# The weight sums of the first pair on VectorE, moved behind the outputs of one product of the down projection and behind the activation sums

## Chip, cores, metric

One core of a Trainium2 chip runs the whole kernel. The metric is device time in microseconds for one execution, on that core. Times of one kernel are compared with runs of the kernel before made on the same chip in the same rounds. A profile is one execution of the same program.

## The reference, cut to what matters

```python
x = A_x                                    # 2048 rows of 1024, bfloat16
h = x + attention(layernorm(x)) @ wo       # sliding, dilated, 32 heads
n = layernorm(h)
h2 = h + ((n @ w_gate) * (n @ w_up)) @ w_down   # 1024 -> 3584 -> 1024
```

The second half is the part at issue. Rows are handled in chunks of 512. Chunk 0 is computed plainly. Chunk 1's down projection, and the gate, up and down projections of chunks 2 and 3 together, use a Strassen-like scheme: seven products of quarter blocks instead of eight, at the price of sums and differences of blocks on the other engines.

## The kernel before

The place where the change is made lies at two thirds of the span. Chunk 1's down projection ends there, and the pairs of gate and up products for chunks 2 and 3 begin. Products accumulate in tiles called ex and ey (two of each) in PSUM, the memory into which the matmuls write; `dprod` is a product, 14 matmuls for each tile:

```python
def result(c, rows, t, hf, ps, sc, other, lo=0, n=TC):
    cols = bass.ds(hf * 512 + lo, n)
    nc.vector.scalar_tensor_tensor(rows[:, cols], ps[:, bass.ds(lo, n)], sc,
                                   rows[:, cols] if other is None else other[:, bass.ds(lo, n)], ALU.mult, ALU.add)   # L792
    nc.sync.dma_start(outf[bass.ds(c * TC + t * 128, 128), cols], rows[:, cols])                                      # L794
```

For pair 0, the scaled weights are made by ScalarE and the four weight sums by VectorE (GpSimd makes those of all other pairs):

```python
def weight_sums(n, eng=nc.gpsimd):
    raw = pair["w", n]
    wt = wpool.tile([128, KO, 2, 256], F16, tag="w", name=f"ws_{n}")
    if n == 0:
        nc.scalar.activation(wt[:], raw[:], ACTF.Copy, scale=scale_gu.s)              # L654
    else:
        nc.vector.tensor_scalar(wt[:], raw[:], scale_gu.s, None, ALU.mult)            # L656
    sw = wpool.tile([128, 2, 4, 4, 128], F16, tag="w", name=f"sw_{n}")
    # ... a11, a21, a12, a22 are quarters of wt
        eng.tensor_tensor(sw[:, i, 0], a21, a22, ALU.add)                             # L661
        eng.tensor_tensor(sw[:, i, 1], sw[:, i, 0], a11, ALU.subtract)                # L662
        eng.tensor_tensor(sw[:, i, 2], a11, a21, ALU.subtract)                        # L663
        eng.tensor_tensor(sw[:, i, 3], a12, sw[:, i, 1], ALU.subtract)                # L664
```

The activation sums read the transposed, normalized rows of both chunks, l2 (chunk 2) and l3 (chunk 3), which the DMA queue transposes in eight transfers (in the profile of before they are issued one after the other, the last at 507.7 us, and that one lands 3.3 us later):

```python
def activation_sums(l2, l3, room):
    b11, b12, b21, b22 = l2[:, 0:4, :], l3[:, 0:4, :], l2[:, 4:8, :], l3[:, 4:8, :]
    # ... t1 to t4 are parts of room (the tile prodx)
    nc.vector.tensor_tensor(t1, b12, b11, ALU.subtract)                               # L672
    nc.vector.tensor_tensor(t2, b22, t1, ALU.subtract)                                # L673
    nc.vector.tensor_tensor(t3, b22, b12, ALU.subtract)                               # L674
    nc.vector.tensor_tensor(t4, b21, t2, ALU.subtract)                                # L675
```

And the order in which they are called, which is the order on each engine (the kernel schedules by hand):

```python
for t in range(4):
    ln_rows(3, t, l3)                      # ScalarE makes a row block, the DMA queue transposes it (L870)
sub([dn["kx"], dn["vx"]], dn["21"], dn["11"])
weight_sums(0, nc.vector)                  # <- the call that moves
retire(2)
et = att.tile([128, TC], F32, tag="t3", name="et")
for q in range(2):
    dprod(ex[q], q, EF["21"], fcells(dn["12"]), False)
    nc.vector.tensor_tensor(et[:], p5t[:, q, :], hs1[2 + q][:, 512:1024], ALU.add)    # L978
    result(1, hs1[2 + q], 2 + q, 1, ex[q], dn["inv"], et)
retire(1)
activation_sums(l2, l3, dn["px"])
for q in range(2):
    dprod(ey[q], q, EF["12"], fcells(dn["22"]), False)
    nc.vector.tensor_tensor(p5t[:, q, :], p5t[:, q, :], hs1[q][:, 512:1024], ALU.add) # L984
    result(1, hs1[q], q, 1, ey[q], dn["inv"], p5t[:, q, :])
for q in range(2):
    dprod(ex[q], q, EF["22"], fcells([dn["kx"], dn["vx"]]), False)                    # "second ex product"
    result(1, hs1[2 + q], 2 + q, 0, ex[q], dn["inv"], None)
# ... then pair_block(0): groups px, pv, py, pz of four matmuls each
```

The second ex product adds to the same PSUM tile that the first output reads, so it must wait for that output: 3.18 us in the profile of before. In `pair_block(0)` the first pv group takes a PSUM bank that the ey 0 output frees, and the second pv group one that the second output of ex 0 frees: in the profile after the change each of them starts about 0.05 us after that output ends (520.78 after 520.73, 522.89 after 522.83).

## Time and profile before

| | before |
|---|---|
| time, median of 3 runs | 783.46 us (782.1 to 784.1) |
| span of the profile | 779.9 us |
| TensorE busy | 766.8 us, 98% |
| longest wait of TensorE for another engine | 3.2 us, at the second ex product |
| longest wait of VectorE nearby | 4.44 us, for ScalarE's scaling |

In the timelines each row is start, duration, engine, line, operation, output, inputs, shape and count; a bracket at the end is idle time of the engine just before the row and what ended it. A matmul of 512 columns lasts 0.379 us but starts 0.216 us after the one before it, so rows of TensorE overlap and distances are best taken from start to start.

### The profile page before, as it was taken

How to read it: one execution, taken by the hardware profiler on the slowest of the kernel's cores; microseconds unless marked ns; L12 is line 12 of the kernel's file. 1: busy time of each engine (PE TensorE's matmuls, PEld its weight loads, DVE VectorE, ACT ScalarE, POOL GpSimd, SP SyncE). 2: the span in 40 equal slices, each digit the busy share in tenths (PEclk: the TensorE clock that was granted, in tenths of full speed). 3: DMA queues.
4: the chain of work that ended last, by engine and by line, in shares of the span. 5: the costliest groups of instructions: out<-in, count | busy, mean ns of one | idle time of the engine just before them, and what ended most of it. 6: DMA issues, size and time to landing. Idle time of an engine off the chain costs nothing.

```text
span 779.9 us, 10436 instructions
## 1 busy us (share of the span) xinstructions
PE 766.8 (98%) x3648; PEld 355.0 (46%) x3707; DVE 614.9 (79%) x805; ACT 473.5 (61%) x1028; POOL 142.4 (18%) x152
## 2 busy tenths in 40 slices
PE   8999999999999999999999999989999999999997
PEld 6544444444444444444444444434444444444444
DVE  6629999999899998999979989975553444579862
ACT  5627445313576652966769799836677677788240
POOL 0000000010000200002000001008778677600000
PEclk9999999999999999999999999999999999999999
DMA  8999693896955868858555492824332323730001
GB/s 272 260 236 209 169 274 90 262 274 173 341 174 186 297 215 234 270 189 270 195 163 195 133 313 75 183 74 110 106 99 64 108 67 97 255 123 28 1 27 55
DMA packets 181605, 133.86 MB, mean 172 GB/s; under 512 B 79024, under 2 KB 174384, under 8 KB 179504
## 3 DMA queue, kind: packets, MB, share of 16 engines
q1 hardware_dynamic: 177968, 111.17, 50.1%
q0 software_dynamic: 3584, 22.02, 8.1%
q8 instruction: 29, 0.48, 0.3%
q14 instruction: 24, 0.20, 0.1%
HBM read 104.86 MB, written 22.02 MB: 163 GB/s over the span
## 4 chain that ended last, share of the span: by engine, by line
PE 88%; DVE 9%; ACT 1%; issue 1%; DMA 1%; SPq 0%; DVEq 0%
PE ps L392 20%; PE pu L392 12%; PE pg L392 12%; PE dx L787 6%; PE pz L680 6%; PE acc L626 6%; PE py L680 6%; PE px L680 6%; PE wo L513 4%; PE pv L680 3%; PE dy L787 3%; DVE h L834 1%; PE ps L355 1%; PE ex L787 1%; DVE prodx L780 1%
## 5 line engine op out<-in xcount | busy, mean ns | idle before, releaser
L392 PE MATMUL ps<-lnT,w_qkv 128*128 128x512 bf16 x721 | 158.9, 379 | 0.8
L392 PEld LDWEIGHTS <-w_qkv 128*128 128x128 bf16 x736 | 71.9, 98 | 85.9
L392 PE MATMUL pu<-lnT,w_wu 128*128 128x512 bf16 x438 | 105.1, 379 | 0.6
L392 PE MATMUL pg<-lnT,w_wg 128*128 128x512 bf16 x440 | 105.1, 379 | 0.4
L306 ACT CAST sg<-ps 128x512 bf16<-128x512 f32 x96 | 54.8, 590 | 54.4 <-PE ps L392 51.1
L475 DVE TENSOR_TENSOR pv<-vD,at 128x4096 bf16<-128x4096 bf16 x32 | 72.5, 2287 | 0.3
L432 DVE TENSOR_TENSOR prod<-qD,kD 128x4096 bf16<-128x4096 bf16 x32 | 72.3, 2284 | 0.1
L680 PEld LDWEIGHTS <-sw 128*128 128x128 f16 x448 | 43.8, 98 | 53.2 <-issue 0.4
L392 PEld LDWEIGHTS <-w_wg 128*128 128x128 bf16 x448 | 43.8, 98 | 52.9
L392 PEld LDWEIGHTS <-w_wu 128*128 128x128 bf16 x448 | 43.8, 98 | 52.9
L596 ACT CAST us<-pu 128x512 bf16<-128x512 f32 x56 | 33.2, 593 | 41.1 <-PE pu L392 38.7
L680 PE MATMUL px<-lnT,ws 128*128 128x512 bf16 x212 | 53.1, 379 | 0.6
L680 PEld LDWEIGHTS <-ws 128*128 128x128 f16 x336 | 32.9, 98 | 39.6
L626 PE MATMUL acc<-w_wd,gs 128*128 128x512 bf16 x219 | 48.2, 379 | 0.3
L487 POOL DMA_DIRECT2D od<-oD x4 | 2.2, 544 | 252.3 <-DVE oD L485 162.5
L661 POOL TENSOR_TENSOR sw<-ws 128x512 f16<-128x512 f16 x26 | 30.0, 1154 | 87.6 <-PE py L680 80.4
L591 ACT CAST gs<-pg 128x512 bf16<-128x512 f32 x56 | 32.9, 587 | 11.4 <-PE pg L392 9.3
L185 ACT ACTIVATE rs<-mv,eps 128x1 f32<-128x1 f32 (+1 forms) x25 | 7.4, 297 | 50.3 <-DVE mv L182 47.1
L434 DVE TENSOR_TENSOR prod<-prod 128x4096 bf16<-128x4096 bf16 x16 | 36.6, 2288 | 0.3
L541 ACT ACTIVATE junkd<-w_wd 128x512 bf16<-128x512 bf16 x56 | 34.3, 613 | 0.0
L626 PEld LDWEIGHTS <-gs 128*128 128x128 bf16 x224 | 21.9, 98 | 26.4
L697 ACT COPY py<-px 128x512 f32<-128x512 f32 x28 | 16.0, 570 | 29.6 <-PE px L680 29.6
(304 smaller groups left out, 1398.0 us busy)
## 6 DMA issues: line engine op xcount, KB each, us to landing
w_wg<-in_B_w_gate_dram SPq DMA_DIRECT2D x14, 1024.0 KB, 6.6
w_wu<-in_B_w_up_dram SPq DMA_DIRECT2D x14, 1024.0 KB, 5.3
w_wd<-in_B_w_down_dram SPq DMA_DIRECT2D x8, 896.0 KB, 7.4
w_pair<-in_B_w_gate_dram SPq DMA_DIRECT2D x14, 512.0 KB, 4.0
w_pair<-in_B_w_up_dram SPq DMA_DIRECT2D x14, 512.0 KB, 5.2
w_wo<-in_A_wo_dram SPq DMA_DIRECT2D x6, 1024.0 KB, 8.4
w_qkv<-in_A_wqkv_dram SPq DMA_DIRECT2D x5, 1024.0 KB, 9.1
kd<-sg SPq DMA_DIRECT2D x32, 144.0 KB, 2.9
```

What stands on the lines that cost most here:

```text
L306: nc.scalar.copy(sg[:, HB:HB + TC], ps[:])
L392: nc.tensor.matmul(ps[:], lhsT=wt[:, ko, bass.ts(j, 128)], rhs=rhs[:, ko, :], start=(ko == 0), stop=(ko == KO - 1))
L432: nc.vector.tensor_tensor(prod[:, j], qD[:], kD[:, :, o:o + SUB], ALU.mult)
L434: nc.vector.tensor_tensor(prod[:, :, 0:16], prod[:, :, 0:16], prod[:, :, 16:32], ALU.add)
L475: nc.vector.tensor_tensor(pv[:, j], vD[:, :, o:o + SUB], at[:, w, None, :].to_broadcast((128, DH, SUB)), ALU.mult)
L513: nc.tensor.matmul(ps[:], lhsT=oTs[c][:, kk, t, :], rhs=wts["wo", c, hf][:, kk, :], start=(kk == 0), stop=(kk == KO - 1))
L541: nc.scalar.activation(junk, src, ACTF.Abs, accum_out=self.l1[:, k:k + 1])
L591: nc.scalar.copy(gs[:], pg[:])
L596: nc.scalar.copy(us[:], pu[:])
L626: nc.tensor.matmul(acc[t][:], lhsT=hT[f][:, bass.ts(t, 128)], rhs=wts["wd", c, hf, b][:, j, :], start=(f == 0), stop=(f == NF - 1))
L680: nc.tensor.matmul(ps[:], lhsT=lhs[:, ko, :], rhs=rhs[:, ko, :], start=(fresh and ko == 0), stop=(ko == 3), skip_group_check=not fresh)
L787: nc.tensor.matmul(ps[:, bass.ds(lo, n)], lhsT=lhs[k][:, bass.ts(q, 128)], rhs=rhs[k][:, bass.ds(lo, n)], start=(fresh and k == 0), stop=( ...
```

## The change

The intent is to let the outputs of the ex product, which need nothing from the weight scaling, go ahead of the weight sums, which do. The call moves behind the activation sums as well. No operation is added or removed.

```diff
     sub([dn["kx"], dn["vx"]], dn["21"], dn["11"])
-    weight_sums(0, nc.vector)
     retire(2)
     et = att.tile([128, TC], F32, tag="t3", name="et")
     for q in range(2):
@@
     retire(1)
     activation_sums(l2, l3, dn["px"])
+    weight_sums(0, nc.vector)
     for q in range(2):
         dprod(ey[q], q, EF["12"], fcells(dn["22"]), False)
```

## The prediction

> **What bounds the kernel now.** I read the page first, then the waits of TensorE over the whole span, then the chain of work that ended last, then the timelines of TensorE, VectorE, ScalarE and the DMA queue around the edited lines. From the page:
>
> ```profile
> span 779.9 us, 10436 instructions
> ...
> PE 766.8 (98%) x3648; PEld 355.0 (46%) x3707; DVE 614.9 (79%) x805; ACT 473.5 (61%) x1028; POOL 142.4 (18%) x152
> ...
> PEclk9999999999999999999999999999999999999999
> ```
>
> TensorE is busy 98% of the span at full clock, so only its 13 us of idle time can be won by a change that removes no matmul. The list of waits says where TensorE stands still for another engine (columns: us in total, times, longest):
>
> ```profile
> PE ex L787 <- DVE h L792: 3.2, 1, 3.2
> PE warm_ps L300 <- DVE warm L286: 1.2, 1, 1.2
> ...
> PE pv L680 <- DVE h L792: 0.2, 1, 0.2
> ```
>
> The longest wait of TensorE in the whole kernel is one of 3.2 us, for the output instruction at line 792; it is the one the change is about. The 0.2 us at the bottom is a few microseconds later in the same stage. TensorE's timeline there (start, duration, engine, line, what, and in brackets the idle time before):
>
> ```profile
> 509.70 1.67 PE L787 MATMUL ey<-lx,gs 128*128 128x512 f16 x7
> 514.56 1.67 PE L787 MATMUL ex<-kx,gs 128*128 128x512 f16 x7 [3.18 <-DVE h L792]
> ```
>
> and VectorE's:
>
> ```profile
> 503.96 2.02 DVE L780 TENSOR_TENSOR vx<-w_dn,w_dn 128x3584 f16<-128x3584 f16 x1
> 510.42 0.69 DVE L661 TENSOR_TENSOR sw<-ws 128x1024 f16<-128x1024 f16 x1 [4.44 <-ACT ws L654]
> ...
> 512.96 0.68 DVE L978 TENSOR_TENSOR et<-ep,h 128x512 f32<-128x512 f32 x1
> 513.75 0.75 DVE L792 SCALAR_TENSOR_TENSOR h<-ex,inv_h1d,et 128x512 bf16<-128x512 f32 x1
> ...
> 516.00 1.22 DVE L672 TENSOR_TENSOR prodx<-lnT,lnT 128x2048 f16<-128x2048 bf16 x1
> ...
> 520.67 0.68 DVE L984 TENSOR_TENSOR ep<-ep,h 128x512 f32<-128x512 f32 x1
> 521.45 0.75 DVE L792 SCALAR_TENSOR_TENSOR h<-ey,inv_h1d,ep 128x512 bf16<-128x512 f32 x1
> ```
>
> What to see: VectorE is itself idle for 4.44 us, 505.98 to 510.42, because the first weight sum (line 661) needs the scaled weights that ScalarE makes in one 3.69 us instruction. Behind it, in VectorE's order, stand the two outputs of the product ex, which finished on TensorE near 505.3. The next product of the program accumulates into the same ex tile and must let the output read it first. So the chain is: ScalarE's scaling, four weight sums, one add, one output, and only then TensorE. The add and output needed nothing from the scaling.
>
> [...] the add at 512.96 had its inputs before 506 and still waited behind line 661. [...] the trace has 1216 to 1226 ns for lines 672 to 675[...]. [...] That matters for the transposes that line 672 reads: they show 1.28 us in the queue but 3.3 us from issue to landing.
>
> **The change part by part.** It removes and adds no instruction. The four sums move from ahead of the ex outputs to behind the four activation sums (lines 672 to 675). The built program's order confirms that only those four rows move on VectorE; ScalarE, GpSimd and the DMA queue keep their order, and the buffer that the sums are written to costs no new wait before they start.
>
> First part, the gain. VectorE is free at 505.98, so add and output for ex 0 take the place of the idle time: start to end from the old row, 512.96 to 514.50, is 1.54 us, so ex 0 is free at 507.5 and ex 1 (start of add at 514.54, end of output at 516.08) at about 509.1. TensorE's last ey group issues at 509.70 and seven matmuls take 1.51 us from start to start (508.19 to 509.70), so the next product may start at 511.21 with no wait. It started at 514.56: TensorE is 3.35 us earlier.
>
> Second part, what takes part of it back. Line 672 waits for all eight transposes of the normalized rows:
>
> ```profile
> 495.64 13.36 SPq L870 DMA_TRANSPOSE lnT<-lnr  x8
> ...
> 506.69 3.69 ACT L654 ACTIVATE ws<-w_pair,sbgu 128x4096 f16<-128x4096 bf16 x1
> ...
> 520.60 1.89 PE L680 MATMUL px<-lnT,ws 128*128 128x512 bf16 x7
> ...
> 522.32 1.03 PE L680 MATMUL pv<-prodx,sw 128*128 128x512 f16 x4
> ...
> 524.37 1.02 PE L680 MATMUL pv<-prodx,sw 128*128 128x512 f16 x4 [0.16 <-DVE h L792]
> ```
>
> These lines are from the timeline of all engines. The last of the eight is issued at 507.7 and lands 3.3 us later, at 511.0. Before, that was hidden (line 672 ran at 516.0). Now VectorE reaches line 672 at about 509.1 and must stand until 511.0. [...] two or three checks, 0.1 us each between lines 792 and 672 in the chain, follow the one that lands last; I put the start at 511.25. The rest is start to start from the old rows: activation sums 516.00 to 520.67 are 4.67 us, so 515.92; weight sums 510.42 to 512.96 are 2.54 us, so 518.46. Then come add and output for ey 0 (520.67 to 522.20, 1.53 us: 519.99), ey 1 (to 523.66, 2.99 us: 521.45), and the second output of ex 0 (to 524.33, 3.66 us: 522.12).
>
> TensorE meanwhile: second ex product 511.21 plus 6.04 (514.56 to 520.60) is 517.25, the px group 1.73 more is 518.98. The first pv needs a PSUM bank that the ey 0 output frees: 520.05, a wait of 1.1 us. Pv and py take 1.73 us, to 521.78. The second pv needs the bank of ex 0: 522.16, a wait of 0.4 us. Before, it started at 524.37. The gain is 524.37 - 522.16 = 2.2 us. In sum: 3.5 us of the old delays (3.35 + 0.15) less 1.5 us of new ones, about 2.1.
>
> Third part, the rest of the kernel. From the second pv on, all that follows hangs on VectorE's outputs or on TensorE, in the same order and at the same distance: scaling of pair 1 on VectorE, the GpSimd sums after it (eight of 1.16 us, 9.4 us of a pair's 12.1), the loads of pair 2. I expect them to move earlier by the same 2.2 us. After this stage TensorE waits for VectorE only 0.6 and 0.3 us, both within the last product, so the shift reaches the end.
>
> **The rivals.** (1) The whole 3.5 us. It would come if the transposes landed before 509.1. What speaks against it is 507.7 plus 3.3 us. The time would be 780.0. (2) Nothing: VectorE is the bound through this stage, and reordering it only swaps which wait TensorE pays. For it speaks that VectorE works without a gap from 510.42 to 525; against it, that 4.44 us of idle time ahead of that shrink to about 2.2. The time would be 783.4. (3) The outputs are stored earlier, right behind the transposes on the same DMA queue, and their 128 KB each slow the last transposes, which now set the time. The DMA engines are full to 510.3, so a few tenths are possible; the gain would be 1.5 us and the time 782. (4) A later bound gives it back, such as GpSimd's sums for pair 1, which end only about 0.7 us before their last user. They keep that distance unless VectorE's part moves less than TensorE's; I count on 0.3 us at most.
>
> **Range and chances.** The median of before is 783.46, so 783.46 - 2.2 = 781.3 us. The runs of before spread over 2.0 us (782.1 to 784.1), almost as much as the gain, so the range is mostly noise: 779.9 to 782.6. Two per cent are 15.7 us; neither the largest gain here (3.5) nor any loss I can construct comes near it: faster 0.005, same 0.99, slower 0.005.
>
> **What would show it.** Right: no wait of TensorE before the second ex product; a VectorE wait near 2 us before line 672, ended by a transpose; two new TensorE waits before the two pv groups, about 1.1 and 0.4 us, ended by line 792; the px group near 517.3 and the second pv near 522.2; after that every row 2.2 us earlier. Wrong: a VectorE wait at line 672 under 0.5 us (rival 1), a second pv near 524 (rival 2), transposes landing after 511.5 (rival 3), or waits of TensorE between pairs that were not there (rival 4).

That the sums cost the same in their new place is then the author's estimate, made from their old rows; in both profiles the activation sums take 4.67 us from start to start and the weight sums 2.54 us.

## The result, and the profile after

| | before | after |
|---|---|---|
| time, median of 4 runs each | 783.59 us (782.1 to 784.1) | 779.9 us (779.55 to 780.23) |
| ratio, 95% interval | 1 | 0.9956 (0.9939 to 0.9973) |
| span of the profile | 779.9 us | 778.4 us |

A ratio here is the mean time of one kernel's fast runs over that of the other's fast runs of the same rounds, so it isn't quite the ratio of the medians. The change gains some 3.4 us, clear of noise and far inside 2%. The prediction was 781.3 us; the measured median lies on the very bottom of its range, 779.9.

VectorE's timeline after, same columns as before:

```profile
506.80 0.68 DVE L977 TENSOR_TENSOR et<-ep,h 128x512 f32<-128x512 f32 x1
...
511.98 1.23 DVE L672 TENSOR_TENSOR prodx<-lnT,lnT 128x2048 f16<-128x2048 bf16 x1 [2.05 <-DMA out_dram<-h]
...
516.65 0.69 DVE L661 TENSOR_TENSOR sw<-ws 128x1024 f16<-128x1024 f16 x1
...
519.98 0.75 DVE L792 SCALAR_TENSOR_TENSOR h<-ey,inv_h1d,ep 128x512 bf16<-128x512 f32 x1
```

The add of ex 0 now starts right after the subtractions, 506.80, and the 4.44 us wait for ScalarE is gone. In its place is a new wait of 2.05 us before the first activation sum. TensorE's timeline after:

```profile
510.61 1.67 PE L787 MATMUL ey<-lx,gs 128*128 128x512 f16 x7
512.12 1.67 PE L787 MATMUL ex<-kx,gs 128*128 128x512 f16 x7
...
518.16 1.89 PE L680 MATMUL px<-lnT,ws 128*128 128x512 bf16 x8
520.78 1.02 PE L680 MATMUL pv<-prodx,sw 128*128 128x512 f16 x4 [0.73 <-DVE h L792]
...
522.89 1.02 PE L680 MATMUL pv<-prodx,sw 128*128 128x512 f16 x4 [0.22 <-DVE h L792]
```

The second ex product follows the ey product with no wait: 510.61 to 512.12 is the 1.51 us that seven matmuls take. Two small waits have appeared before the pv groups. And the DMA queue after:

```profile
496.48 13.40 SPq L870 DMA_TRANSPOSE lnT<-lnr  x8
509.98 13.88 SPq L794 DMA_DIRECT2D out_dram<-h  x6
```

To compare stages I take the time from the first matmul of the first ex product (499.13 before, 500.03 after) to the second pv group (524.37 and 522.89). It is 25.24 us before and 22.86 us after: the stage gained 2.4 us. From the second pv group to the end of the span it is 255.5 us in both. The rest of the difference between these two profiles is at the start: this profile of after came into the stage 0.9 us later.

That leaves a puzzle: the stage explains 2.4 us, but the medians differ by 3.7. The experiments had to settle both the mechanism within the stage and this remainder.

### The profile page after: what moved, and what is told of

Same layout as the page of the kernel before. It is cut to its first block, busy times and chain, and to the rows that moved or that the text cites. A ratio compares the mean times of both kernels' runs of the same rounds, so it can differ in the third digit from the quotient of the medians.

```text
span 778.4 us, 10494 instructions
## 1 busy us (share of the span) xinstructions
PE 771.1 (99%) x3707; PEld 355.4 (46%) x3707; DVE 615.0 (79%) x805; ACT 473.3 (61%) x1028; POOL 142.3 (18%) x152
## 4 chain that ended last, share of the span: by engine, by line
PE 88%; DVE 9%; DMA 1%; ACT 1%; SPq 0%; issue 0%; DVEq 0%
PE ps L392 20%; PE pg L392 12%; PE pu L392 12%; PE dx L787 6%; PE pz L680 6%; PE acc L626 6%; PE py L680 6%; PE px L680 6%; PE wo L513 4%; PE pv L680 3%; PE dy L787 3%; DVE h L834 1%; PE ps L355 1%; DMA w_qkv<-in_A_wqkv_dram 1%; PE ex L787 1%; DVE prodx L780 1%
## 5 line engine op out<-in xcount | busy, mean ns | idle before, releaser
L680 PE MATMUL px<-lnT,ws 128*128 128x512 bf16 x224 | 55.2, 379 | 0.0
L626 PEld LDWEIGHTS <-gs 128*128 128x128 bf16 x224 | 21.9, 98 | 26.4
```

Source lines behind the costliest of these rows:

```text
L626: nc.tensor.matmul(acc[t][:], lhsT=hT[f][:, bass.ts(t, 128)], rhs=wts["wd", c, hf, b][:, j, :], start=(f == 0), stop=(f == NF - 1))
L680: nc.tensor.matmul(ps[:], lhsT=lhs[:, ko, :], rhs=rhs[:, ko, :], start=(fresh and ko == 0), stop=(ko == 3), skip_group_check=not fresh)
```

## The experiments

**Theory A**: VectorE works its queue in order (in the profile of before the add of ex 0 came 6.98 us after the subtractions, behind the weight sums; in that of after it follows them with no wait). What counts is when the outputs of ex and ey leave it, and the new wait there is for the last transposes. **Rivals**: the activation sums themselves hold the pv groups; the output stores hold line 672; something outside the stage gained as well.

### Both kernels again

No edit. Five rounds each, to size the change and the noise.

> The changed kernel once more, unaltered, to size the change in more rounds. In the first profiles the stage (from the first ex product of the 21 block to the second pv group) is 2.4 us shorter than before (22.86 against 25.24 us), but the medians differ by 3.7 us. Theory A (all of the gain is in this stage): ratio 0.9969, give or take 0.0007, and the stage again 22.9 us with TensorE waits of about 0.7 and 0.2 us before the two pv groups. Theory B (something outside the stage gained as well): ratio near 0.9955 and another part of the timeline shorter than in the profile of before.

> The kernel before, unaltered, timed against itself: the noise of the method. Ratio 1.000; if the ratio is off by more than 0.0007 then differences of half a microsecond cannot be told in five rounds. Its profile should have the 3.18 us wait of TensorE before the second ex product again, and the 4.44 us wait of VectorE for the scaling.

Measured: after 780.14 us (ratio 0.9961, interval 0.9947 to 0.9975), stage 22.74 us, with waits of 0.61 and 0.23 us before the two pv groups. The interval holds the ratios of both theories, so the times alone decide nothing. Before against itself: 783.78 us, ratio 1.0002 (0.9989 to 1.0014), with the waits of 3.19 and 4.44 us again. The profile of before, taken again, brought the surprise. Its stage was not 25.24 but 26.60 us. TensorE's timeline of this second profile of before:

```profile
510.47 1.67 PE L787 MATMUL ey<-lx,gs 128*128 128x512 f16 x7
515.34 3.14 PE L787 MATMUL ex<-kx,gs 128*128 128x512 f16 x7 [3.19 <-DVE h L792]
518.28 1.92 PE L787 MATMUL ex<-vx,gs 128*128 128x512 f16 x7
```

The same seven matmuls that took 1.51 us from start to start in the first profile took 2.94 us here. The table of stretches of the same execution (stretch, length, busy time of each engine, then the granted TensorE clock, as a share of full speed, and the DMA share and rate) tells why; the column to read is the third from the end:

```profile
515.00:516.00 1.00, 0.66 (x2) 0.25 (x2) 0.96 (x2) 0.00 (x0) 0.00 (x0) 0.67 0.00 0
516.00:517.00 1.00, 1.00 (x4) 0.29 (x2) 0.90 (x3) 0.00 (x0) 0.00 (x0) 0.50 0.39 131
517.00:518.00 1.00, 1.00 (x4) 0.44 (x3) 1.00 (x1) 0.00 (x0) 0.00 (x0) 0.50 0.23 81
518.00:519.00 1.00, 1.00 (x5) 0.32 (x3) 0.97 (x1) 0.00 (x0) 0.00 (x0) 0.62 0.15 50
519.00:520.00 1.00, 1.00 (x6) 0.44 (x5) 1.00 (x2) 0.00 (x0) 0.00 (x0) 1.00 0.00 0
```

Right after the wait the clock is at half. The missing shares add up to 0.33 + 0.50 + 0.50 + 0.38 = 1.71 us, that is 3.4 us at half clock. The mean clock listed for this execution is 0.998, and 1.71 us are 0.002 of its 782.1 us. The first profile of before showed 1.00 over the whole of this stage: it happened to be an execution in which the clock stayed up.

```profile
514.00:516.00 2.00, 1.44 (x7) 0.68 (x7) 1.86 (x3) 0.00 (x0) 0.00 (x0) 1.00 0.19 66
516.00:518.00 2.00, 2.00 (x11) 0.88 (x9) 1.97 (x3) 0.00 (x0) 0.00 (x0) 1.00 0.23 74
```

Each run also lists its mean granted clock, and 3.4 us at half clock are 0.002 of it. Over all 35 executions of the kernel before with a listed clock, the 27 with 0.998 or less took 783.8 us on average, the 8 with 0.999 or more 782.3 us. All nine executions of the changed kernel stand at 0.999 or more, at 780.1 us on average. (For executions without a profile the drop is inferred from the mean clock, not seen. Four of the 27 stand at 0.996 and took 784.7 us on average: their clock was down for longer, and no profile shows where.) So a **clock theory** was added: the wait of TensorE also makes its clock drop in most executions, and the change gains that too.

### Half the change: the sums between the ex outputs and the activation sums

```diff
     retire(1)
-    activation_sums(l2, l3, dn["px"])
     weight_sums(0, nc.vector)
+    activation_sums(l2, l3, dn["px"])
```

(against the changed kernel)

> Only half of the change: the weight sums stand behind the ex outputs but stay ahead of the activation sums. Theory A (VectorE's queue is in order and stands about 2 us for the last transposes at line 672, while the scaled weights come 0.7 us earlier than those): the weight sums fill that time, start about 1.3 us after the ex outputs end, line 672 starts with no wait, the waits of TensorE before the two pv groups fall from 0.73 and 0.22 to about 0.2 and 0.1 or none; stage 22.2 us, 0.7 us faster than the changed kernel, ratio to before 0.9961. Theory C (the place behind the activation sums is what gains): the 3.18 us wait or a good part of it is back and the time lies near that of before.

Measured: 779.7 us, ratio 0.9953 (0.994 to 0.9965), stage 22.21 us. VectorE's timeline:

```profile
511.84 0.69 DVE L661 TENSOR_TENSOR sw<-ws 128x1024 f16<-128x1024 f16 x1 [1.38 <-ACT ws L654]
...
514.38 1.22 DVE L672 TENSOR_TENSOR prodx<-lnT,lnT 128x2048 f16<-128x2048 bf16 x1
```

and TensorE's two pv groups:

```profile
520.64 1.02 PE L680 MATMUL pv<-prodx,sw 128*128 128x512 f16 x4
...
522.76 1.02 PE L680 MATMUL pv<-prodx,sw 128*128 128x512 f16 x4 [0.23 <-DVE h L792]
```

The weight sums fill the time in which the transposes land, and line 672 starts with no wait, as theory A says. Of the two waits of TensorE the first is nearly gone, but the second, expected to fall from 0.22 to about 0.1 us or none, is still 0.23 us: a miss. The stage fell by 0.5 to 0.65 us against the two profiles of after (expected 0.7); the times' intervals overlap, so the step is shown by the profile and not by the clock on the wall. What gains in the change is its first half, getting out of the way of the ex outputs. Its second half, going behind the activation sums too, costs a little.

### Also the adds of the ey outputs moved ahead

```diff
+    for q in range(2):
+        nc.vector.tensor_tensor(p5t[:, q, :], p5t[:, q, :], hs1[q][:, 512:1024], ALU.add)
     weight_sums(0, nc.vector)
     activation_sums(l2, l3, dn["px"])
     for q in range(2):
         dprod(ey[q], q, EF["12"], fcells(dn["22"]), False)
-        nc.vector.tensor_tensor(p5t[:, q, :], p5t[:, q, :], hs1[q][:, 512:1024], ALU.add)
```

(against the kernel of the last experiment)

> Like the last, and the two adds ahead of the ey outputs (0.6 us each, their inputs long there) also moved into VectorE's idle time ahead of the weight sums. Theory A: no wait of TensorE is left in the stage, the second pv group starts right behind the first py group, stage 21.9 us, 1.0 us faster than the changed kernel and 3.4 us than before, ratio to before 0.9957. Theory D (the pv groups wait for the activation sums themselves, not for a bank freed by the outputs): the two pv waits stay as in the last kernel.

Measured: 778.72 us (778.57 to 779.4), ratio 0.994 (0.9928 to 0.9953): the lowest median of a correct version, 1.4 us below the changed kernel in the same rounds (a later version, at 778.98 us in other rounds, can't be told from it). The stage is 21.59 us (21.9 expected). VectorE and TensorE:

```profile
510.96 0.69 DVE L661 TENSOR_TENSOR sw<-ws 128x1024 f16<-128x1024 f16 x1 [0.19 <-ACT ws L654]
```

```profile
520.38 1.03 PE L680 MATMUL py<-prodx,sw 128*128 128x512 f16 x4
521.24 1.03 PE L680 MATMUL pv<-prodx,sw 128*128 128x512 f16 x4
```

VectorE's idle time before the sums shrank from 1.38 to 0.19 us, and the second pv group follows the first py group at the plain distance of 0.86 us: no wait is left. The pv groups waited for the banks that the outputs free, not for the activation sums: these end later here than in the changed kernel (near 518.2 us, against 516.7), and yet the pv groups start earlier. That rival falls.

### Keeping TensorE busy in the old wait

```diff
+    fill = psum.tile([128, TC], F32, tag="mm", name="fill")
+    for i in range(13):
+        nc.tensor.matmul(fill[:], lhsT=ones[:], rhs=scale_d.rowb[:].to_broadcast((128, TC)), start=True, stop=True)
     for q in range(2):
         dprod(ex[q], q, EF["22"], fcells([dn["kx"], dn["vx"]]), False)
```

(against the kernel before)

> The kernel before, with 13 matmuls of constants into an unused bank (13 x 0.216 = 2.8 us) put into the wait of TensorE ahead of the second ex product; nothing reads them and VectorE's work is unchanged. Of 15 executions of the kernel before seen so far, the 10 with a mean granted clock of 0.998 or less took 783.9 us on average, the 5 with 0.999 or more 782.6. Clock theory: the idle time of 3.2 us makes the clock drop to half for a few microseconds in most executions, costing 1.4 us; kept busy it never drops: all executions at 0.999 or more, second ex product still starting where it did, time 782.6, ratio 0.9985. Rival (the clock follows something else, or is noise): ratio 1.000 and clocks as mixed as before.

Measured: 782.12 us, ratio 0.9984 (0.9971 to 0.9996). All six executions have a mean clock of 0.999 or more, and average 782.2 us; of the 11 of before in these rounds eight are at 0.998 or less. TensorE's timeline:

```profile
512.01 2.99 PE L988 MATMUL fill<-rowbd,ones 128*128 128x512 bf16 x13
515.38 1.67 PE L787 MATMUL ex<-kx,gs 128*128 128x512 f16 x7 [0.37 <-DVE h L792]
```

Thirteen useless matmuls make the kernel 1.3 us faster. The stage is 25.26 us, that of the undropped profile of before (25.24), so nothing else in it moved. The clock theory is confirmed by intervention, and its rival (the clock has another cause) falls. The other runs agree: of the 33 executions of the versions without the old wait, the changed kernel among them, none has a mean clock below 0.999.

### Six fillers, and one add hoisted

How short must the wait be? With `range(6)` in place of `range(13)` (the later of the two runs):

> How short must the wait be for the clock to stay up? The kernel before with 6 filler matmuls and not 13, so TensorE is idle for about 1.9 us before the second ex product (13 left 0.37 us and no drop in 6 executions; 2.4 us of wait in the run with one add early dropped it in 3 of 6). If 1.9 us is short enough: all executions at 0.999 or more and 782.2 us, ratio 0.9985. If half the drops remain: clocks mixed, about 783, ratio 0.9995.

Measured: 782.02 us, ratio 0.9981 (0.9968 to 0.9994); one execution of five at 0.998 (783.31 us), four at 1.0 (781.9 us on average). Neither expectation holds to the letter: mostly up, not always. The wait in the profile is 1.88 us:

```profile
514.12 1.67 PE L787 MATMUL ex<-kx,gs 128*128 128x512 f16 x7 [1.88 <-DVE h L792]
```

The earlier run is the kernel before with one add taken out from behind the sums:

```diff
+    et = att.tile([128, TC], F32, tag="t3", name="et")
+    nc.vector.tensor_tensor(et[:], p5t[:, 0, :], hs1[2][:, 512:1024], ALU.add)
     weight_sums(0, nc.vector)
     retire(2)
-    et = att.tile([128, TC], F32, tag="t3", name="et")
     for q in range(2):
         dprod(ex[q], q, EF["21"], fcells(dn["12"]), False)
-        nc.vector.tensor_tensor(et[:], p5t[:, q, :], hs1[2 + q][:, 512:1024], ALU.add)
+        if q == 1:
+            nc.vector.tensor_tensor(et[:], p5t[:, q, :], hs1[2 + q][:, 512:1024], ALU.add)
```

> The kernel before, with only the first add of the ex outputs hoisted ahead of the weight sums, into VectorE's idle time: 0.62 to 0.79 us less between the sums and the first ex output. TensorE's wait is then about 2.5 us instead of 3.2. Order theory alone: all later work on VectorE 0.6 us earlier, so 0.6 us, ratio 0.9992. With the clock theory: 2.5 us is too short to drop the clock (or does it less often), so up to 0.6 + 0.9 = 1.5 us, ratio 0.998, and granted clocks of 0.999 or more.

Measured: 781.9 us, ratio 0.9985 (0.9969 to 1.0). The stage is 24.44 us, 0.8 less than before, and the wait 2.38 us:

```profile
514.44 1.67 PE L787 MATMUL ex<-kx,gs 128*128 128x512 f16 x7 [2.38 <-DVE h L792]
```

The expectation on the clock was a miss: three of six executions still dropped (at 0.997 and 0.998: 783.1 us on average, against 781.4 for the other three). Within each of the two states the gain is 0.8 to 0.9 us over all executions of before, and 0.5 to 0.8 us over those of the same rounds (dropped 783.8, up 781.9 us). That is the order's own part; 0.6 us was expected. I can't give a limit below which the clock is safe: the drop was inferred in 27 of 35 executions at 3.2 us of wait, 3 of 6 at 2.4, 1 of 5 at 1.9, 0 of 6 at 0.4. These come from different rounds and chips: at 3.2 us it was 8 of 11 in the rounds of the 2.4 us run and 9 of 9 in those of the 1.9 us run, so that 2.4 us is safer than 3.2 is not shown.

### The cause of the old wait taken away instead

The order of before is kept, and VectorE scales the weights of pair 0 too:

```diff
-    if n == 0:
+    if n < 0:
         nc.scalar.activation(wt[:], raw[:], ACTF.Copy, scale=scale_gu.s)
     else:
         nc.vector.tensor_scalar(wt[:], raw[:], scale_gu.s, None, ALU.mult)
```

> The order of the kernel before is kept, and what VectorE waited for is taken away instead: the scaling of pair 0's weights is done by VectorE itself (1.27 us, as for the other pairs) and not by ScalarE (3.69 us, after the rows). If the cause of the old wait is the scaling that stood ahead of the outputs in VectorE's queue: first ex output at 1.27 + 2.54 + 1.54 = 5.35 us after the subtractions end, about when TensorE has finished the ey product; TensorE's wait 0.1 to 0.2 us, stage 22.1 us (3.1 less than before), no clock drop, time about 779.4, ratio 0.995. If something else held the outputs, the wait stays.

Measured: 778.98 us, ratio 0.9943 (0.993 to 0.9955), all six executions at 0.999 or more, stage 22.11 us (22.1 expected). VectorE's and TensorE's timelines:

```profile
505.87 1.29 DVE L656 TENSOR_SCALAR ws<-w_pair,sbgu 128x4096 f16<-128x4096 bf16 x1
507.26 0.69 DVE L661 TENSOR_TENSOR sw<-ws 128x1024 f16<-128x1024 f16 x1
```

```profile
509.68 1.67 PE L787 MATMUL ey<-lx,gs 128*128 128x512 f16 x7
511.40 1.67 PE L787 MATMUL ex<-kx,gs 128*128 128x512 f16 x7
```

With the sums still ahead of the outputs, TensorE's wait is down to 0.2 us (1.72 us from start to start, not 1.51). So the old wait came from the 3.69 us of ScalarE that the sums waited for. Moving the sums hides that wait; giving the scaling to the engine that needs it removes it, and gains as much or more with one condition changed.

### What ends the new wait at line 672

The profile names a store of an output. That can't be taken at face value: the profile has this store landing at 511.96 us, the last event before line 672 starts at 511.98, but line 672 reads nothing that the store writes. The run is the changed kernel with its first two stores issued after those of ey (the first `result` of ex without its store; the stores behind the ey loop):

> The changed kernel, with the two stores of the first ex outputs issued after those of the ey outputs. The profile names a store of an output as what ended VectorE's wait of 2.05 us at line 672; I think [...] that the last transpose (issued 3.3 us before) ends the wait. Then the wait stays at 2.0 us and the time at that of the changed kernel (ratio 0.9958). Rival: the store, or its traffic, holds line 672: the wait falls below 1.5 us or moves.

Measured: 780.0 us, ratio 0.9957 (0.9939 to 0.9975), stage 22.94 us. VectorE and the DMA queue:

```profile
511.98 1.22 DVE L672 TENSOR_TENSOR prodx<-lnT,lnT 128x2048 f16<-128x2048 bf16 x1 [2.13 <-DMA lnT<-lnr]
```

```profile
496.49 13.38 SPq L870 DMA_TRANSPOSE lnT<-lnr  x8
520.75 1.81 SPq L794 DMA_DIRECT2D out_dram<-h  x2
```

With no store under way until 520.75, line 672 starts at 511.98 as before, and now the profile names the transposes. The stores neither hold nor slow it. (Why the profile named the store isn't shown.) To show that it is the last four transposes, the changed kernel with the activation sums made from l2 alone:

```diff
-    b11, b12, b21, b22 = l2[:, 0:4, :], l3[:, 0:4, :], l2[:, 4:8, :], l3[:, 4:8, :]
+    b11, b12, b21, b22 = l2[:, 0:4, :], l2[:, 0:4, :], l2[:, 4:8, :], l2[:, 4:8, :]
@@
-    pair["b"] = (b11, b21, t1, t2, t3, t4, b22)
+    pair["b"] = (b11, b21, t1, t2, t3, t4, l3[:, 4:8, :])
```

> Wrong result on purpose: the changed kernel with the activation sums made from chunk 2's rows alone, so that line 672 needs four transposes that landed long before and not the last four; all instructions, sizes and their order are the same. If the last transposes are what VectorE waits 2 us for, the wait at line 672 is gone; line 661 then waits at most for the scaled weights, which come before the four activation sums end, so everything after on VectorE is 2.0 us earlier, both waits of TensorE before the pv groups (0.73 and 0.22 us) vanish, and the time falls by 0.9 us below the changed kernel: about 779.2, ratio 0.9946 to 0.995. If the pv waits were for something else they stay.

Measured: 778.38 us, ratio 0.9931 (0.9916 to 0.9946), stage 21.58 us. The comparison with the reference still passed, presumably because the second half adds too little to the rows for its tolerance to see this error; it is no valid kernel all the same. VectorE and TensorE:

```profile
509.74 1.22 DVE L672 TENSOR_TENSOR prodx<-lnT 128x2048 f16<-128x2048 bf16 x1
```

```profile
518.05 1.89 PE L680 MATMUL px<-lnT,ws 128*128 128x512 bf16 x7
519.78 1.03 PE L680 MATMUL pv<-prodx,sw 128*128 128x512 f16 x4
...
521.50 1.03 PE L680 MATMUL pv<-prodx,sw 128*128 128x512 f16 x4
```

Both the 2 us wait of VectorE and the two pv waits of TensorE are gone, and the stage is as short as that of the version with the adds moved. The time fell by more than the expected 0.9 us against the earlier runs of after; these were other rounds, so I rest on the stage (22.74 and 22.86 to 21.58).

## Why the prediction was right, and where a term was missing

- **Gain at the second ex product.** Predicted: no wait, product earlier by 3.35 us. Right: the wait is gone. Less the 0.9 us by which this profile entered the stage later, the product starts at 511.22; predicted was 511.21.
- **The new wait at line 672.** Predicted: near 2 us, ended by the last transpose. Measured 2.05 us. Taking the label at face value would have refuted it; two experiments showed that the transposes end it.
- **The pv waits.** Predicted 1.1 and 0.4 us, measured 0.73 and 0.22 us in the profile's idle column. From start to start against the 1.73 us of the groups before, they are 0.89 and 0.38 us. The small excess came from line 672, which I put at 511.25 and which started at 511.08 on the clock of before.
- **The px and second pv groups.** Predicted 517.25 and 522.16. Measured, less 0.9 us: 517.26 and 521.99. The prediction's second sum, "3.5 us ... less 1.5 us ..., about 2.1", gives 2.0 as written: it adds 0.15 us of the idle column to distances from start to start. From start to start the old delay of the second pv group was 0.32 us (524.37 - 522.32 - 1.73), and the sum then agrees with the 2.2 us.
- **The rest moves along.** Right: 255.5 us from the second pv group to the end in both profiles.
- **The size.** Predicted 2.2 us. That is the gain over the executions of before whose clock stayed up: 782.3 - 780.1 = 2.2 us. Over all of them it is 783.5 - 780.1 = 3.4 us. The step that failed is in "Range and chances": "The runs of before spread over 2.0 us ..., so the range is mostly noise". Part of that spread was two states, 1.5 us apart, and the slower is over three times as frequent. The term left out of the sum is 27/35 of 1.5 us, about 1.2 us: the drop of the clock that the old wait caused and the change removes. I had read "at full clock" from a line in tenths of one fortunate execution, in which 3.4 us at half clock couldn't have shown anyway (1.71 us missing of a slice of 19.5 us leave 0.91, still a 9). That the time still came out inside the range is luck: the low end was set for noise, and the median of four lies on it, while the next five executions had 780.14 us.
- **Rivals.** (1) fell: the transposes land later than VectorE is ready. (2) fell: the second pv group starts 2.4 us earlier in the stage. (3) fell with the late stores. (4) fell with the unchanged rest of the span.

What stays open is how the clock decides: why 3.2 us of idle time mostly drops it (by the mean clock, in 27 of 35 executions) and sometimes doesn't, and what sets the 3.4 us at half clock of the one drop seen in a profile. No run shows it.

## What to carry to other kernels

On an engine that works its queue in order, as VectorE did here, look at each wait for what stands behind it that needs nothing from what it waits for; put that ahead, and place what waits for the latest arrival last. Price an idle stretch of TensorE at its own length plus the half-clock time that may follow it: here, after 3.2 us of idle time, 1.5 us more in about three executions of four (27 of 35). And take a second profile of the kernel before, beside every run's mean clock, before calling a spread of 0.3% noise.
